# An attention and maxout kernel: columns in token order, and one store per output tile of 128 rows

## The chip, the cores and the metric

The kernel runs on one core of one Trainium2 chip. The metric is the device time of one execution, in microseconds (us). "Before" is the kernel as it stood, "after" the same kernel with the change.

## What is computed

```python
def _attn_ref(q, k, v):                        # q, k, v: 8 x 12 x 448 x 64, float32
    scale = 1.0 / np.sqrt(q.shape[-1])
    scores = scale * np.matmul(q, k.transpose(0, 1, 3, 2))
    m = np.max(scores, axis=-1, keepdims=True)
    e = np.exp(scores - m)
    attn = e / (np.sum(e, axis=-1, keepdims=True) + np.exp(-m) + 1e-09)
    return np.matmul(attn, v).astype(np.float32)

def _moe_ref(x, w1, w2, w3, w_out):            # x: 3584 x 768, all weights 768 x 768
    h = np.maximum(np.maximum(x @ w1, x @ w2), x @ w3)
    return (h @ w_out).astype(np.float32)

# reference: x = the attention's output, one row for each (batch, token), the 12 heads side by side
```

Softmax has one added to its denominator in the unshifted form: e^s / (sum of e^s + 1).

## The kernel before, in words

**Attention.** Eight batches of 448 tokens, each with 12 heads in three groups of four: 24 groups. A group's q, k and v are loaded so that partition p holds the seven tokens 7p to 7p+6 of a head (`rows_of`), and the kernel works through seven "chunks" j, where chunk j holds the tokens 7p+j. So in every tile whose columns are queries, column j*64+p belongs to token 7p+j: the columns are in chunk order. For each group TensorE makes the scores (`visit`, L297), ScalarE the exponentials (L321), VectorE the sums over chunks (`sum_e`, L331), and TensorE the denominators (`den_group`) and the products with v (`num_group`, L345). `norm_group` (L400, VectorE) then multiplies the product, in PSUM, by the reciprocal of the denominator, and writes 448 columns of `xT[b]`, the transposed x of batch b in fp16: twice for each group. The three groups of batch 0 run in two parts of three and four chunks, and `num_part` (L493) writes their x.

**Feed-forward.** `hT`, a tile of fp16 for two batches (896 columns), holds the transposed h. `up_piece` makes 448 columns of it for one block of 128 features and one of the three weights: six matmuls, then an eviction that copies (first weight) or takes the maximum in place (L523, L526). `up_part` does it for batch 0 by parts, two feature blocks at a time (matmuls L537, evictions L546 and L548). `out_piece` makes 128 rows by 384 columns of the output: matmuls of six h blocks (L560 for batch 0, L786 when mixed into the later attention), an eviction that divides by 256 into `o_sb` (L568 or L576), and after the second half `store` (L586). The attention's steps and the pieces are mixed by hand-written lists and by a planner that books costs in steps; TensorE executes its queue strictly in that order.

**The store.** A tile of 128 columns of h holds two runs of 64 columns in chunk order, so `store` issues two transfers of 64 rows, and the rows of each lie seven apart in the output:

```python
for n in range(2):
    b, j = divmod(2 * t + n, NJ)
    rows = out[(b0 + b) * S : (b0 + b + 1) * S].rearrange("(p j) m -> j p m", j=NJ)
    engines[n].dma_start(out=rows[j][:, cols], in_=src[half(n)])
```

**The end.** The last four batches are made in two pairs by a scheme of seven products for eight (`late_pair`; matmuls L1038). `out_unit(m)` gives two output tiles, `o1` (tile m) and `o2` (tile 3+m), in halves of 384 columns. Its `put` evicts a half from PSUM: on ScalarE (L1162), on VectorE with a temporary added (L1168), or, where `late` is set in the last pair, on VectorE without one (L1164). In the last pair many halves are stored as soon as they are evicted; of the two transfers, the first is issued on SyncE and the second on GpSimd or, where `late` is set, on ScalarE. `last_tile` makes tile 6 of a pair with plain matmuls (L1240) and evicts it on VectorE (L1212); in the last pair its second half comes as two quarters, and its second transfers are on ScalarE. The order of all this is one written list that ends with the last pair's unit D[2] and tile e.

SyncE's queue carries, besides the stores, 16 transposing transfers of q and k (L288). GpSimd issues all other loads.

Of the kernel before, what the change touches and what calls it, by code (L numbers as in the profile page):

```python
# [13 lines left out]
ALU = mybir.AluOpType  # L14
ts = bass.ts

MMDT = FP16
LAMBDA = 256.0
# [4 lines left out]
def kernel(  # L23
# [11 lines left out]
    nc = tc.nc  # L35

    B, H, S, D = q.shape
    NTOK, DM = out.shape
    DFF = moe_w1.shape[1]
    KC = 64  # L40
    NJ = S // KC
# [29 lines left out]
    banks = ExitStack()  # L71
# [9 lines left out]
    def single(name, shape=(512,), dtype=FP32):  # L81
        return ps1.tile([128, *shape], dtype, tag="bank1", name=name)
# [21 lines left out]
    def half(n):  # L104
        return slice(n * KC, n * KC + KC)
# [54 lines left out]
    for _ in range(WQ):  # L160
        for r in range(2):
            for c in range(2):
                nc.tensor.matmul(
                    out=warm[r][c * KC : c * KC + KC, 0:WN],
# [25 lines left out]
    state = {}  # L190
# [8 lines left out]
    def book(engine, cost, ready=0.0):  # L199
        given[engine] = max(given[engine], ready, steps[0]) + cost  # L200
        return given[engine] + SEEN
# [135 lines left out]

    xT = {}

    def new_x(b):  # L340
        xT[b] = xt_pool.tile([128, NDC, S], MMDT, tag="xT", name="xT")

# [54 lines left out]
    def norm_group(i, banks, r):  # L397
        book("dve", 2.8)
        b, g = groups[i]
        nc.vector.tensor_tensor(  # L400
            out=xT[b][:, 2 * g + r, :], in0=banks[r][:, 0:S], in1=state[i]["rb"][:, r], op=ALU.mult
        )


# [95 lines left out]
    hT = {}  # L500
# [27 lines left out]
    def up_part(b, fp, i, part, bank=None):  # L528
        if fp == 0 and i == 0 and part == 0:
            hT[b // 2] = ht_pool.tile([128, NFC, 2 * S], MMDT, tag="hT", name="hT")  # L530
        q0, q1 = PARTS[part]
        nq = (q1 - q0) * KC
        dst = hT[b // 2][:, 2 * fp : 2 * fp + 2, q0 * KC : q1 * KC]
        p_i = single("p_i") if bank is None else bank
        for j in range(2):
            for dc in range(NDC):
                nc.tensor.matmul(  # L537
                    out=p_i[:, ts(j, nq)],
                    lhsT=w_sb[i][:, dc, ts(2 * fp + j, 128)],
                    rhs=xT[b][:, dc, q0 * KC : q1 * KC],  # L540
                    start=(dc == 0),
                    stop=(dc == NDC - 1),
                )
        src = p_i[:, 0 : 2 * nq].rearrange("p (j q) -> p j q", j=2)
        if i == 0:
            nc.vector.tensor_copy(out=dst, in_=src)  # L546
        else:
            nc.vector.tensor_tensor(out=dst, in0=dst, in1=src, op=ALU.max)  # L548

    NH = 2  # L550
    NW = DM // NH
    NT = 2 * S // 128
# [26 lines left out]
        if nh == NH - 1:  # L579
            store(2 * bp, t, o_sb, slice(0, DM))  # L580

    def store(b0, t, src, cols, engines=(nc.sync, nc.sync)):
        for n in range(2):
            b, j = divmod(2 * t + n, NJ)
            rows = out[(b0 + b) * S : (b0 + b + 1) * S].rearrange("(p j) m -> j p m", j=NJ)
            engines[n].dma_start(out=rows[j][:, cols], in_=src[half(n)])  # L586

    pieces = []

# [54 lines left out]
    for i, part in ((0, 0), (1, 0), (0, 1), (1, 1), (2, 0), (2, 1)):  # L644
        for fp in range(NFC // 2):
            pieces.append((up_part, (0, fp, i, part), 1.0))
# [96 lines left out]
    late = []  # L743
# [230 lines left out]
    for i in range(MID, NI + 1):  # L974
        for op, j, w in ORDER if i > MID else ORDER[4:]:
# [23 lines left out]
            if op == "N":  # L999
                for_pair()  # L1000
                pair = num_group(i - 1)
                n = turn[0] % 2
                steps[0] += 7
                t = max(steps[0] + 1, state[i - 1]["recip"])
# [6 lines left out]
    while spare:  # L1011
        f, a = spare.pop(0)
# [19 lines left out]
    def part(name, n):  # L1032
        return tail.tile([128, n], FP32, tag=name, name=name, bufs=3 if name == "p7" else 4)

    def product(u, which, lhs, rhs, n, start):
        bank = u[which][:, 0:n]
        for k in range(3):
            nc.tensor.matmul(  # L1038
                out=bank,
                lhsT=lhs(k),  # L1040
                rhs=rhs(k),
                start=start and k == 0,
                stop=k == 2,
                skip_group_check=True,
            )
        return bank

    def bank_of(u, which):
        u[which] = tps[taken[0] % 8].tile([128, 512], FP32, tag="tbank", name="bank_" + which)
        taken[0] += 1  # L1050

    def late_pair(p):

        b0 = 2 * p
        ending = p == B // 2 - 1
# [91 lines left out]
        def out_unit(m):  # L1147
            t = comb[3]
            u = {}
            r0 = slice(m * 128, m * 128 + 128)  # L1150
            r1 = slice(NT3 + m * 128, NT3 + m * 128 + 128)

            def copy(name, bank):
                u[name] = part(name, S)[:, 0:NW]
                nc.scalar.activation(out=u[name], in_=bank, func=AF.Copy, scale=1.0 / LAMBDA)

            def put(o, nh, bank, other=None, late=m == 2 and ending):

                engines = nc.sync, nc.scalar if late else nc.gpsimd
                dst = u[o][:, ts(nh, NW)]  # L1160
                if other is None and not late:
                    nc.scalar.activation(out=dst, in_=bank, func=AF.Copy, scale=1.0 / LAMBDA)  # L1162
                elif other is None:
                    nc.vector.tensor_scalar(  # L1164
                        out=dst, in0=bank, scalar1=1.0 / LAMBDA, scalar2=None, op0=ALU.mult
                    )
                else:
                    nc.vector.scalar_tensor_tensor(  # L1168
                        out=dst, in0=bank, scalar=1.0 / LAMBDA, in1=other, op0=ALU.mult, op1=ALU.add
                    )  # L1170
                t = {"o1": m, "o2": 3 + m}[o]
                if ending and (o == "o1" or m == 0):
                    store(b0, t, dst, ts(nh, NW), engines)
                elif nh == (1 if o == "o1" else 0):
                    store(b0, t, u[o], slice(0, DM), engines if ending else (nc.sync, nc.sync))

            def p1():
                bank_of(u, "a")
                copy("p1", product(u, "a", lambda k: hp[:, k, r0], lambda k: wout_sb[:, k, 0:NW], NW, True))

            def p2():
                bank_of(u, "s")
                u["o1"] = tail.tile([128, DM], FP32, tag="o1", name="o1", bufs=5)
                bank = product(u, "s", lambda k: hp[:, 3 + k, r0], lambda k: wout_sb[:, 3 + k, 0:NW], NW, True)
                put("o1", 0, bank, u["p1"], False)

            def p6():
                copy("u2", product(u, "a", lambda k: sh[1][:, k, r0], lambda k: t[:, 1, k], NW, False))

            def p7():  # L1190
                copy("p7", product(u, "s", lambda k: sh[2][:, k, r0], lambda k: t[:, 2, k], NW, True))

            def p5():
                u["o2"] = tail.tile([128, DM], FP32, tag="o2", name="o2", bufs=3)
                put("o2", 1, product(u, "a", lambda k: sh[0][:, k, r0], lambda k: t[:, 0, k], NW, False), u["p7"])

            def p4():
                put("o2", 0, product(u, "s", lambda k: hp[:, 3 + k, r1], lambda k: t[:, 3, k], NW, False), u["u2"])

            def p3():  # L1200
                bank = product(u, "a", lambda k: sh[3][:, k, r0], lambda k: wout_sb[:, 3 + k, NW:DM], NW, False)
                put("o1", 1, bank, late=ending and m > 0)

            return [p1, p2, p6, p7, p5, p4, p3]

        def last_tile():

            o_last = tail.tile([128, DM], FP32, tag="o_last", name="o_last")

            def columns(c0, c1, cuts, end=None):  # L1210
                def done(bank):
                    nc.vector.tensor_scalar(  # L1212
                        out=o_last[:, c0:c1],
                        in0=bank[:, 0 : c1 - c0],
                        scalar1=1.0 / LAMBDA,
                        scalar2=None,
                        op0=ALU.mult,
                    )
                    if end is not None:
                        store(b0, NT - 1, o_last[:, end], end, (nc.sync, nc.scalar if ending else nc.sync))  # L1220

                return plain(hp, NT - 1, c0, c1, cuts, done)

            return (
                columns(0, NW, (3,), slice(0, NW) if ending else None)
                + columns(NW, NW + NW // 2, ())
                + columns(NW + NW // 2, DM, (), slice(NW if ending else 0, DM))
            )
# [54 lines left out]
    g = last_tile()  # L1283
# [61 lines left out]
```

## Time and profile before

| What | Value |
| --- | --- |
| median of 3 runs | 315.86 us (315.54, 315.86, 320.21) |
| the profiled execution | 315.63 us |
| its span in the profile | 313.9 us |
| TensorE matmuls, busy | 300.7 us (96% of the span) |
| VectorE, busy | 247.7 us (79%) |
| ScalarE, busy | 230.7 us (73%) |
| GpSimd, busy | 83.0 us (26%) |
| bytes moved by transfers | 40.58 MB |
| granted TensorE clock | 0.999 |

The span is the time from the first to the last thing that the profile records; the execution's own time is 1.73 us longer. In the profile's rows PE is TensorE's matmuls, PEld its weight loads, DVE VectorE, ACT ScalarE, POOL GpSimd, and SPq and ACTq the queues of SyncE and ScalarE where they issue transfers. A row of a group names line, engine, operation, what it writes and reads, and the number of instructions, then the total busy time in us and the mean of one in ns, then the idle time before them and what ended it. A row of a wait has the waiter, what it waited for, the total in us, the number of times and the longest. A row of the timeline begins with start and duration in us.

### The profile page before, as it was taken

The numbers are of one execution on the slowest core, as the hardware profiler recorded it, in microseconds if no ns is written. First come the engines' busy times: TensorE is split into PE (matmuls) and PEld (weight loads), VectorE is DVE, ScalarE is ACT, GpSimd is POOL, SyncE is SP. The second block draws the span as 40 slices with busy tenths as digits, with TensorE's granted clock in tenths as the row PEclk, the third lists the DMA queues.
The fourth block names the chain that finished last, engine by engine and source line by source line (L and its number), as shares of the span: only waits on it lengthen the run. The fifth ranks groups of instructions, "written<-read, shape, count | busy, mean of one in ns | idle before, by whom it ended". The sixth has DMA issues, their size and how long they took to land.

```text
span 313.9 us, 11772 instructions
## 1 busy us (share of the span) xinstructions
PE 300.7 (96%) x5132; PEld 213.2 (68%) x5132; DVE 247.7 (79%) x456; ACT 230.7 (73%) x315; POOL 83.0 (26%) x137
## 2 busy tenths in 40 slices
PE   7779999999999999999999999999999999999992
PEld 5557777658999778777666767777765555556551
DVE  3667598999889788888887898877857994989753
ACT  1999859987888988889888899999845457451540
POOL 8644441220434333434332434010000000000220
PEclk9999999999999999999999999999999999999999
DMA  8999999699778999889999999950004000002687
GB/s 152 196 203 205 208 207 203 102 158 176 95 118 138 188 210 143 99 127 180 204 150 145 100 194 217 143 90 2 4 2 102 1 2 0 0 2 70 179 241 215
DMA packets 59348, 40.58 MB, mean 129 GB/s; under 512 B 32256, under 2 KB 56288, under 8 KB 59296
## 3 DMA queue, kind: packets, MB, share of 16 engines
q0 software_dynamic: 25104, 21.80, 47.8%
q1 hardware_dynamic: 33648, 17.21, 26.6%
q8 instruction: 40, 0.66, 0.8%
q10 hardware_dynamic: 544, 0.82, 0.8%
q14 instruction: 12, 0.10, 0.1%
HBM read 42.47 MB, written 11.01 MB: 170 GB/s over the span
## 4 chain that ended last, share of the span: by engine, by line
PE 85%; ACT 6%; DVE 3%; issue 2%; DMA 1%; DVEq 0%; ACTq 0%
PE piece L786 35%; PE bank_a L1038 11%; PE stp L297 9%; PE bank_s L1038 8%; PE av L345 8%; PE p_i L537 4%; ACT eTp L419 3%; PE bank_a L1240 2%; PE piece L537 2%; ACT eT L321 2%; PE den L345 2%; DMA first_k<-in_k_dram 1%; PE piece L560 1%; DVE eS L331 1%; PE num L345 1%
## 5 line engine op out<-in xcount | busy, mean ns | idle before, releaser
L321 ACT ACTIVATE eT<-stp 128x896 f16<-128x896 f32 x147 | 128.9, 920 | 20.5 <-PE stp L297 20.4
L786 PE MATMUL piece<-xT,w 64*64 64x448 f16 x1968 | 120.6, 349 | 0.4 <-DVE xT L400 0.3
L786 PEld LDWEIGHTS <-w 64*64 64x64 f16 x1968 | 76.8, 107 | 18.1 <-issue 1.1
L331 DVE TENSOR_TENSOR eS<-eS,eT 128x896 f16<-128x896 f16 x105 | 64.9, 618 | 3.4 <-ACT eT L321 0.2
L297 PE MATMUL stp<-qkT 64*64 64x448 f16 (+2 forms) x756 | 63.4, 334 | 3.0 <-issue 0.9
L526 DVE TENSOR_TENSOR hT<-hT,piece 128x448 f16<-128x448 f16 x52 | 32.2, 619 | 13.1 <-PE piece L786 8.1
L297 PEld LDWEIGHTS <-qkT 64*64 64x64 f16 x756 | 28.6, 105 | 17.4 <-issue 6.8
L345 PE MATMUL av<-eT,ld_v 64*64 64x448 f16 x588 | 32.2, 349 | 0.0
L400 DVE TENSOR_TENSOR xT<-av,rb 128x448 f16<-128x448 f32 x42 | 24.2, 618 | 8.3 <-PE av L345 6.9
L345 PEld LDWEIGHTS <-ld_v 64*64 64x64 f16 x756 | 26.1, 107 | 6.5 <-issue 0.5
L114 POOL DMA_DIRECT2D ld_v<-in_v_dram x28 | 16.8, 600 | 51.5 <-PE stp L297 31.7
L786 PE MATMUL piece<-w,hT 64*64 64x384 f16 x456 | 29.3, 323 | 0.1
L586 POOL DMA_DIRECT2D out_dram<-o x7 | 3.8, 538 | 93.7 <-DVE o L1168 92.1
L114 POOL DMA_DIRECT2D ld_k<-in_k_dram x26 | 15.4, 596 | 39.1 <-PE stp L297 34.7
L365 ACT ACTIVATE rb<-den 128x896 f32<-128x896 f32 x21 | 19.3, 917 | 8.2 <-PE den L345 8.1
L419 ACT ACTIVATE eTp<-stp 128x768 f16<-128x768 f32 (+3 forms) x24 | 18.1, 821 | 6.0 <-PE stp L297 5.9
L537 PEld LDWEIGHTS <-w 128*128 128x128 f16 x216 | 18.7, 98 | 5.0 <-issue 3.5
L1038 PEld LDWEIGHTS <-comb 128*128 128x128 f16 x132 | 12.9, 98 | 12.2 <-issue 0.4
L786 PEld LDWEIGHTS <-hT 64*64 64x64 f16 x456 | 18.5, 107 | 3.7 <-issue 0.3
L372 ACT ACTIVATE rb<-rb 128x896 f32<-128x896 f32 x21 | 20.0, 952 | 0.2
L537 PE MATMUL p_i<-xT,w 128*128 128x192 f16 (+1 forms) x156 | 16.5, 257 | 0.0
L114 POOL DMA_DIRECT2D ld_q<-in_q_dram x26 | 15.7, 616 | 1.1 <-issue 1.1
(103 smaller groups left out, 404.9 us busy)
## 6 DMA issues: line engine op xcount, KB each, us to landing
out_dram<-o_sb SPq DMA_DIRECT2D x28, 192.0 KB, 4.6
ld_v<-in_v_dram POOLq DMA_DIRECT2D x28, 112.0 KB, 4.1
ld_k<-in_k_dram POOLq DMA_DIRECT2D x26, 112.0 KB, 3.0
ld_q<-in_q_dram POOLq DMA_DIRECT2D x26, 112.0 KB, 4.0
out_dram<-o SPq DMA_DIRECT2D x14, 192.0 KB, 3.1
ld_q<-in_q_dram POOLq DMA_DIRECT2D x11, 224.0 KB, 9.2
ld_k<-in_k_dram POOLq DMA_DIRECT2D x10, 224.0 KB, 9.3
ld_v<-in_v_dram POOLq DMA_DIRECT2D x10, 224.0 KB, 8.5
```

The source lines that it names most:

```text
L114: return eng.dma_start(out=dst[half(hp)].rearrange("p s j d -> p s (j d)"), in_=rows_of(name, i)[half(hp)])
L297: mm = nc.tensor.matmul(out=out[half(c), r], lhsT=qkT[half(r), 0, j, h], rhs=qkT[half(r), 1, q0:q1, h], start=True, stop=True,)
L321: nc.scalar.activation(out=st["eT"][:, j], in_=stp[:, :, 0:S], func=AF.Exp, scale=scale, bias=-math.log(EDIV))
L331: nc.vector.tensor_tensor(out=st["eS"], in0=st["eT"][:, 0] if j == 1 else st["eS"], in1=st["eT"][:, j], op=ALU.add,)
L345: nc.tensor.matmul(out=outs[r][half(c)], lhsT=weights(r, c), rhs=moving(r, c), start=start, stop=stop,)
L372: nc.scalar.activation(out=st["rb"], in_=st["rb"], func=AF.Exp, bias=math.log(LAMBDA), scale=-1.0)
L400: nc.vector.tensor_tensor(out=xT[b][:, 2 * g + r, :], in0=banks[r][:, 0:S], in1=state[i]["rb"][:, r], op=ALU.mult)
L419: nc.scalar.activation(out=eT[:, j0 : j0 + n].rearrange("p j r q -> p r j q"), in_=stp[:, :, 0 : n * nq].rearrange("p r (j q) -> p r j q", ...
L526: nc.vector.tensor_tensor(out=dst, in0=dst, in1=p_i[:, 0:S], op=ALU.max)
L537: nc.tensor.matmul(out=p_i[:, ts(j, nq)], lhsT=w_sb[i][:, dc, ts(2 * fp + j, 128)], rhs=xT[b][:, dc, q0 * KC : q1 * KC], start=(dc == 0), ...
L786: nc.tensor.matmul(out=p["bank"][half(c), 0:w], lhsT=lhs(k, r, c), rhs=rhs(k, r), start=(r == p["first"] and k == 0), stop=(r != p["first" ...
L1038: nc.tensor.matmul(out=bank, lhsT=lhs(k), rhs=rhs(k), start=start and k == 0, stop=k == 2, skip_group_check=True,)
```

## The change

- `norm_group` writes the columns of x in the order of the tokens: column q*7+j in place of j*64+q. The values and the operation stay; the write becomes seven runs of 64 elements, each with a step of seven elements.
- `num_part` still writes batch 0's x in chunk order; `up_part` turns the order when it evicts h, for `hT[0]`.
- Everything behind (sums of x and h, matmuls, evictions of the output) keeps its instructions, on columns that are now in token order.
- `store` issues one transfer of 128 rows, which lie one behind the other in the output, on SyncE.
- In the last pair, `put` evicts every half without a temporary on ScalarE, where two were on VectorE. Tile 5 (the `o2` of m = 2) is stored in two halves, not whole. GpSimd stores nothing any more, and ScalarE issues one store: the second half of tile 2.

```diff
--- before.py
+++ after.py
@@ -337,6 +337,11 @@
 
     xT = {}
 
+
+
+    def by_chunk(t):
+        return t.rearrange("p (q j) -> p j q", j=NJ)
+
     def new_x(b):
         xT[b] = xt_pool.tile([128, NDC, S], MMDT, tag="xT", name="xT")
 
@@ -398,7 +403,10 @@
         book("dve", 2.8)
         b, g = groups[i]
         nc.vector.tensor_tensor(
-            out=xT[b][:, 2 * g + r, :], in0=banks[r][:, 0:S], in1=state[i]["rb"][:, r], op=ALU.mult
+            out=by_chunk(xT[b][:, 2 * g + r]),
+            in0=banks[r][:, 0:S].rearrange("p (j q) -> p j q", j=NJ),
+            in1=state[i]["rb"][:, r].rearrange("p (j q) -> p j q", j=NJ),
+            op=ALU.mult,
         )
 
 
@@ -530,7 +538,7 @@
             hT[b // 2] = ht_pool.tile([128, NFC, 2 * S], MMDT, tag="hT", name="hT")
         q0, q1 = PARTS[part]
         nq = (q1 - q0) * KC
-        dst = hT[b // 2][:, 2 * fp : 2 * fp + 2, q0 * KC : q1 * KC]
+        dst = hT[0][:, 2 * fp : 2 * fp + 2, 0:S].rearrange("p f (q j) -> p f j q", j=NJ)[:, :, q0:q1]
         p_i = single("p_i") if bank is None else bank
         for j in range(2):
             for dc in range(NDC):
@@ -541,7 +549,7 @@
                     start=(dc == 0),
                     stop=(dc == NDC - 1),
                 )
-        src = p_i[:, 0 : 2 * nq].rearrange("p (j q) -> p j q", j=2)
+        src = p_i[:, 0 : 2 * nq].rearrange("p (f j q) -> p f j q", f=2, q=KC)
         if i == 0:
             nc.vector.tensor_copy(out=dst, in_=src)
         else:
@@ -579,11 +587,8 @@
         if nh == NH - 1:
             store(2 * bp, t, o_sb, slice(0, DM))
 
-    def store(b0, t, src, cols, engines=(nc.sync, nc.sync)):
-        for n in range(2):
-            b, j = divmod(2 * t + n, NJ)
-            rows = out[(b0 + b) * S : (b0 + b + 1) * S].rearrange("(p j) m -> j p m", j=NJ)
-            engines[n].dma_start(out=rows[j][:, cols], in_=src[half(n)])
+    def store(b0, t, src, cols, engine=nc.sync):
+        engine.dma_start(out=out[b0 * S + t * 128 :][0:128, cols], in_=src)
 
     pieces = []
 
@@ -1154,25 +1159,19 @@
                 u[name] = part(name, S)[:, 0:NW]
                 nc.scalar.activation(out=u[name], in_=bank, func=AF.Copy, scale=1.0 / LAMBDA)
 
-            def put(o, nh, bank, other=None, late=m == 2 and ending):
-
-                engines = nc.sync, nc.scalar if late else nc.gpsimd
+            def put(o, nh, bank, other=None):
                 dst = u[o][:, ts(nh, NW)]
-                if other is None and not late:
+                if other is None:
                     nc.scalar.activation(out=dst, in_=bank, func=AF.Copy, scale=1.0 / LAMBDA)
-                elif other is None:
-                    nc.vector.tensor_scalar(
-                        out=dst, in0=bank, scalar1=1.0 / LAMBDA, scalar2=None, op0=ALU.mult
-                    )
                 else:
                     nc.vector.scalar_tensor_tensor(
                         out=dst, in0=bank, scalar=1.0 / LAMBDA, in1=other, op0=ALU.mult, op1=ALU.add
                     )
                 t = {"o1": m, "o2": 3 + m}[o]
-                if ending and (o == "o1" or m == 0):
-                    store(b0, t, dst, ts(nh, NW), engines)
+                if ending and (o == "o1" or m != 1):
+                    store(b0, t, dst, ts(nh, NW), nc.scalar if t == 2 and nh == 1 else nc.sync)
                 elif nh == (1 if o == "o1" else 0):
-                    store(b0, t, u[o], slice(0, DM), engines if ending else (nc.sync, nc.sync))
+                    store(b0, t, u[o], slice(0, DM))
 
             def p1():
                 bank_of(u, "a")
@@ -1182,7 +1181,7 @@
                 bank_of(u, "s")
                 u["o1"] = tail.tile([128, DM], FP32, tag="o1", name="o1", bufs=5)
                 bank = product(u, "s", lambda k: hp[:, 3 + k, r0], lambda k: wout_sb[:, 3 + k, 0:NW], NW, True)
-                put("o1", 0, bank, u["p1"], False)
+                put("o1", 0, bank, u["p1"])
 
             def p6():
                 copy("u2", product(u, "a", lambda k: sh[1][:, k, r0], lambda k: t[:, 1, k], NW, False))
@@ -1199,7 +1198,7 @@
 
             def p3():
                 bank = product(u, "a", lambda k: sh[3][:, k, r0], lambda k: wout_sb[:, 3 + k, NW:DM], NW, False)
-                put("o1", 1, bank, late=ending and m > 0)
+                put("o1", 1, bank)
 
             return [p1, p2, p6, p7, p5, p4, p3]
 
@@ -1217,7 +1216,7 @@
                         op0=ALU.mult,
                     )
                     if end is not None:
-                        store(b0, NT - 1, o_last[:, end], end, (nc.sync, nc.scalar if ending else nc.sync))
+                        store(b0, NT - 1, o_last[:, end], end)
 
                 return plain(hp, NT - 1, c0, c1, cuts, done)
```

## The prediction

> **What bounds the kernel now.** I read the page first: busy shares, then the chain that ended last.
>
> ```profile
> span 313.9 us, 11772 instructions
> PE 300.7 (96%) x5132; PEld 213.2 (68%) x5132; DVE 247.7 (79%) x456; ACT 230.7 (73%) x315; POOL 83.0 (26%) x137
> ...
> PE 85%; ACT 6%; DVE 3%; issue 2%; DMA 1%; DVEq 0%; ACTq 0%
> ```
>
> TensorE is the bound: 96% busy, 85% of the chain. Transfers are 1% of it, although their engines are busy for most of the span. A change pays only if TensorE gets shorter, waits less, or the work after its last matmul ends sooner. Next, the busy time of each engine over the steady stretch and over the last eight microseconds:
>
> ```profile
> core 0: us, PE busy (x) PEld busy (x) DVE busy (x) ACT busy (x) POOL busy (x), PEclk, DMA share, GB/s
> 75.00:225.00 150.00, 149.89 (x3182) 116.83 (x3176) 126.81 (x237) 130.49 (x165) 47.65 (x80) 1.00 0.88 136
> ...
> 306.00:310.00 4.00, 2.15 (x20) 1.51 (x17) 2.43 (x6) 0.00 (x0) 0.00 (x0) 1.00 0.96 267
> 310.00:314.00 4.00, 0.00 (x0) 0.00 (x0) 0.00 (x0) 0.00 (x0) 0.00 (x0) 0.91 0.46 155
> ```
>
> From 75 to 225 us TensorE loses 0.1 us in 150, and VectorE is idle for 23. From 306 on the transfer engines are 96% busy. Third, the waits of TensorE's weight loads, and the group of the instruction that the change alters most:
>
> ```profile
> PEld L297 <- DVE xT L400: 3.0, 11, 0.4
> ```
>
> ```profile
> L400 DVE TENSOR_TENSOR xT<-av,rb 128x448 f16<-128x448 f32 x42 | 24.2, 618 | 8.3 <-PE av L345 6.9 <-ACT eT L321 1.0
> ...
> L493 DVE TENSOR_TENSOR xT<-num,rb 128x256 f16<-128x256 f32 x6 | 2.3, 417 | 1.2 <-ACT rb L466 1.2
> ...
> L493 DVE TENSOR_TENSOR xT<-num,rb 128x192 f16<-128x192 f32 x6 | 1.9, 352 | 2.3 <-ACT rb L466 2.3
> ```
>
> The normalisation comes in pairs (21 of them). In 11 pairs its end is what the next score matmuls wait for (0.27 us each), since it frees their bank: a longer L400 reaches TensorE at once. Last, the end in order of time:
>
> ```profile
> 306.39 0.56 DVE L1168 SCALAR_TENSOR_TENSOR o<-bank_a,p 128x384 f32<-128x384 f32 x1
> 306.87 0.55 DVE L1168 SCALAR_TENSOR_TENSOR o<-bank_s,u 128x384 f32<-128x384 f32 x1
> ...
> 306.98 0.84 SPq L586 DMA_DIRECT2D out_dram<-o_last  x1
> ...
> 307.49 0.66 PE L1240 MATMUL bank_a<-w,hT 128*128 128x192 f16 x6
> 307.69 0.56 DVE L1164 TENSOR_SCALAR o<-bank_a 128x384 f32<-128x384 f32 x1
> 307.91 1.58 SPq L586 DMA_DIRECT2D out_dram<-o  x2
> 308.19 0.36 DVE L1212 TENSOR_SCALAR o_last<-bank_a 128x192 f32<-128x192 f32 x1
> 308.85 1.11 ACTq L586 DMA_DIRECT2D out_dram<-o_last  x1
> 309.68 0.80 SPq L586 DMA_DIRECT2D out_dram<-o_last  x1
> ```
>
> TensorE ends at 308.15, the last eviction at 308.55, but SyncE, still busy with earlier stores, begins the last store at 309.68: 1.13 us late. That store lands 3.4 us after its issue begins, at 313.1; 0.8 us later the span ends.
>
> **The change part by part.** (1) The 42 normalisations (L400) write the same 448 values with a step of 7 fp16 elements, 14 bytes. Reads, count and order stay. The three widths above fit a line: (618-352)/(448-192) = 1.04 ns an element plus 152 ns. So the operation already moves one element per 1.04 ns, and a write of one element at a time may cost the same wherever it lands. No row of this trace writes single elements apart; the bounds are 618 ns and one doubled element time, 618+466 = 1084 ns. I take 618: the row is the same operation at its slow pace, with nothing packed that a step could undo. Upper end: rival D. A gain is excluded, as no work is removed.
>
> [...]
>
> (2) The 18 evictions of batch 0's h (L546, L548) write with the same step, and 12 read it back too. Same bounds: 555 or 680 ns as now, up to 0.4 or 0.53 us more each. I take 0, for the same reason.
>
> (3) One wait is added. Batch 0's first output tile now needs columns from every part of h, so its fifth weight load (line 560) waits for the last maximum:
>
> ```profile
> 59.28 1.14 PE L560 MATMUL piece<-w,hT 128*128 128x384 f16 x6
> ...
> 59.50 0.68 DVE L548 TENSOR_TENSOR hT<-hT,piece 128x512 f16<-128x512 f16 x1
> ```
>
> The six matmuls take 0.19 us each, so the fifth starts at 60.04; the maximum ends at 60.18. TensorE waits 0.15 us, about 0.2 with the signal. Behind it stand the next scores, at 60.35 and for them ScalarE. Bounds 0 (0.3 us of unexplained idle stands before those scores) and 0.7 (the whole operation in front). I take +0.2. The other matmuls keep their order and waits.
>
> (4) Stores. Outside the end, 28 transfers of 64 rows become 14 of 128 on SyncE. The transposes behind them start earlier, but nothing waits for those: no row of TensorE's waits names them. 0. In the end, 26 issues on SyncE, 7 on GpSimd and 5 on ScalarE become 19 on SyncE and 1 on ScalarE. A 64-row issue takes 466 ns at least, 584 median, up to 853. No 128-row store is in the trace; the nearest is one load of the start, 64 rows with two runs each:
>
> ```profile
> L114 SPq DMA_DIRECT2D first_k<-in_k_dram x1: 771/771/771, 0.7 to 0.7; - x1
> ```
>
> I take 0.77 us, bounds 0.47 (cost by instruction) and 1.17 (two median short issues). SyncE's last four stores are ready at 306.29, 306.95, 307.42 and 308.55. At 0.77 they begin at 306.3, 307.1, 307.8 and 308.6: the last is not late, 1.1 us gained. At 1.0 it begins at 309.3, 0.4 gained; at 1.17, at 309.8, 0.1 lost. (The 16 stores from 292.3 on make a second limit, 292.3 plus 15 issues: 303.9 at 0.77, 309.9 at 1.17.) But transfers are nearly saturated there, and the last one carries 192 KB in place of 96. Six halves of 197 KB become ready after 306.2: 1.18 MB at some 300 GB/s are 3.9 us. With about 1 us from ready to moving, bytes flow until some 311.2, against 312.1 now. I take half of the 1.1 us: -0.5, bounds -1.1 and +0.2.
>
> (5) The second halves of the last pair's tiles 1 and 2 (L1164, two) go from VectorE to ScalarE: 0.49 for 0.55 us. ScalarE is idle from 300.86 to 303.05 and after 305.8, which hides both; without that cover they would delay a temporary by 0.5 us. VectorE's last eviction starts at 308.19 as TensorE lets it. 0. The evictions' waits for a free buffer drop one of two transfers; none cost time. 0.
>
> **Sum.** +0.2 - 0.5 = -0.3 us on the profiled execution, 315.63 (span 313.9 and 1.73 around it): 315.3. The median of the runs is 315.86, 0.2 above; the three runs lie 315.54 to 320.21. I give 315.3.
>
> **Rivals.** B, *the saturated end*: store bandwidth and not the late issue sets the end, -0.5 becomes 0, and the wait of (3) stays: 315.8. For it: 96% from 306 to 310. Against: 1.1 us in which a finished tile had not been asked for.
>
> C, *long issues*: a 128-row issue costs more than two short ones, say 1.3 us under load, and SyncE falls behind from 292.3 on: the last store begins at 292.3 + 15 x 1.3 = 311.8, +2.1 for -0.5: 317.9. It decides from 1.16 us. For it: 1109 ns on ScalarE while SyncE issued too. Against: 96 and 192 KB stores both reach 466.
>
> D, *the step halves the element rate*, the other side. Place: L400. Price: 2 x 0.466 = 0.93 us a pair. TensorE waits already in 11 pairs, so at least 10.2; at most 21 x 0.93 = 19.6. (2) adds 18 x 0.45 = 8 us of VectorE, mostly beside idle time. I take 13: 328. It passes 2% (6.3 us) from 0.3 us a pair if all count, 0.57 if 11 do: L400 at 770 to 900 ns. For it: no row shows such a write. Against: the slow pace of the row.
>
> E, *whole tiles drain faster*: the last bytes at the 356 GB/s of the best slices, 1.18 MB in 3.3 us, so 0.6 more: 314.7. For it: the digits of the last slices vary between 169 and 384 GB/s. Against: halves overlap, and 300 GB/s is already reached.
>
> [...]
>
> That the change does less than it says is B.
>
> **How the numbers follow.** Forecast 0.47, B 0.20, C 0.08, E 0.09, D 0.16. Range 313.8 to 318.5: below, the forecast with (4) at its full gain and E, 314.1, and a little; above, C with 0.7 in place of 0.2 for (3), 318.4, which also holds a small cost of the step, up to 0.15 us a pair. It leaves out D, 0.16. Two per cent, 6.3 us, is about what a measurement of this kernel can tell from no change. Only D goes beyond, nearly always: slower 0.15, same 0.83, and 0.02 for a gain over 2%, which no case here gives.
>
> **What would show it.** Right: L400 at 618 ns within 10, its wait row still near 3 us, the last store on SyncE beginning before 309.3, its issue under 1 us, span 313 to 314. Wrong: L400 over 770 and its wait row over 10 us (D); issues of 1.3 us (C); the last store prompt but landing at 313 (B).

## The result, and the profile after

The change made the kernel 28% slower. Medians here and below are of all runs; ratios and their intervals count only the runs in the faster of two states that the executions show.

| | before | after |
| --- | --- | --- |
| median of 6 runs each | 316.66 us | 405.85 us (401.08 to 406.98) |
| ratio, 95% interval | | 1.2785 [1.2704, 1.2865] |
| span of the profiled execution | 313.9 us | 404.0 us |
| granted TensorE clock | 0.999 | 0.916 |

Below are the head of the page of after, its clock digits and the first line of its chain. The lines of the code have moved: L400 is L405, L493 is L501, L537 is L545, L546 and L548 are L554 and L556, L560 is L568, L586 is L591, L786 is L791.

```profile
span 404.0 us, 11725 instructions
PE 335.5 (83%) x5132; PEld 215.4 (53%) x5132; DVE 319.1 (79%) x454; ACT 235.2 (58%) x317; POOL 79.0 (20%) x130
...
PEclk9999968888989888989899889898898899999999
...
PE 60%; DVE 22%; issue 9%; ACT 5%; DMA 2%; POOL 1%; DVEq 0%; POOLq 0%; ACTq 0%
```

VectorE was 3% of the chain and is 22%. TensorE runs the same 5132 matmuls and is busy for 34.8 us longer: the digits of its clock fall to 6 in the sixth slice and are 8 or 9 from there to the end of the attention. The groups whose write the change turned, and one that it left alone (L501), with the mean of one in ns after the comma:

```profile
L405 DVE TENSOR_TENSOR xT<-av,rb 128x448 f16<-128x448 f32 x42 | 76.6, 1988 | 9.4 <-PE av L350 7.8 <-ACT eT L321 1.5
...
L556 DVE TENSOR_TENSOR hT<-hT,piece 128x512 f16<-128x512 f16 x4 | 8.7, 2180 | 1.8 <-PE piece L545 1.8
L556 DVE TENSOR_TENSOR hT<-hT,p_i 128x384 f16<-128x384 f16 x5 | 8.3, 1661 | 0.7 <-PE p_i L545 0.7
...
L501 DVE TENSOR_TENSOR xT<-num,rb 128x256 f16<-128x256 f32 x6 | 2.2, 416 | 0.1
```

Every turned write takes some three times as long: 1988 ns for 618, 1661 for 553, 2180 for 682. The waits of TensorE and of its weight loads (total, times, longest):

```profile
PE stp L297 <- DVE xT L405: 38.0, 17, 2.5
...
PEld L297 <- DVE xT L405: 35.5, 13, 2.9
...
PEld L568 <- DVE hT L556: 4.4, 1, 4.4
```

The score matmuls wait for a bank, 17 times, 2.2 us a time; before, 11 weight loads waited 0.27 us each. Where the 90 us lie is seen in the windows. Each kernel's span is cut at the start of the first normalisation and at the end of the last; the first stretch is the feed-forward of batch 0 between the attention's first groups. Before, then after:

```profile
20.00:58.40 38.40, 37.18 (x710) 28.45 (x705) 29.62 (x54) 32.19 (x41) 14.29 (x21) 1.00 1.17 194
58.40:233.40 175.00, 174.46 (x3630) 133.11 (x3629) 149.37 (x279) 150.36 (x188) 51.46 (x86) 1.00 0.85 132
233.40:313.90 80.50, 74.41 (x449) 41.13 (x443) 58.93 (x103) 34.94 (x67) 3.76 (x7) 1.00 0.28 79
```

```profile
20.00:75.30 55.30, 43.34 (x711) 31.14 (x706) 49.56 (x56) 32.90 (x41) 14.14 (x21) 0.88 0.81 135
75.30:326.90 251.60, 204.82 (x3655) 133.48 (x3653) 202.12 (x279) 153.39 (x188) 51.19 (x86) 0.89 0.59 92
326.90:404.00 77.10, 72.61 (x417) 40.35 (x417) 57.82 (x101) 36.01 (x69) 0.00 (x0) 1.00 0.22 83
```

The three stretches differ by +16.9, +76.6 and -3.4 us, 90.1 in all. In the middle one TensorE's idle time goes from 0.5 to 46.8 us, and its matmuls are busy for 204.8 us in place of 174.5, at a mean clock of 0.89. So there are two losses: 46 us of waiting and 30 us of a slower clock. The first stretch has both too: 10.7 us more idle time and 6.2 us more busy time, at 0.88.

The mean hides how the clock falls. One of the 17 waits, and the clock (the third number from the end) in the two stretches behind it:

```profile
301.86 0.38 PE L297 MATMUL stp<-qkT 64*64 64x448 f16 x4 [2.31 <-DVE xT L405]
```

```profile
302.90:306.10 3.20, 3.20 (x40) 1.74 (x36) 2.49 (x5) 2.04 (x3) 0.00 (x0) 0.50 0.00 0
306.30:316.30 10.00, 7.69 (x168) 4.68 (x163) 7.67 (x10) 5.79 (x7) 0.00 (x0) 1.00 0.01 2
```

From 302.8 to 306.2 us, 3.4 us, the granted clock is half, and then whole again until the next pair. The middle of the span has 16 such stretches. At half speed each loses 1.7 us, by this estimate 27 us of the 30.

The last stretch got shorter. Half of its 3.4 us lies ahead of the last matmul, where fewer matmuls are left (417 records for 449); the other half is the end. In order of time:

```profile
399.29 0.66 PE L1239 MATMUL bank_a<-w,hT 128*128 128x192 f16 x6
...
399.98 0.36 DVE L1211 TENSOR_SCALAR o_last<-bank_a 128x192 f32<-128x192 f32 x1 [0.62 <-PE bank_a L1239]
...
400.37 0.33 SPq L591 DMA_DIRECT2D out_dram<-o_last  x1
```

The last matmul ends at 399.95, the eviction at 400.34, and the last store begins 0.03 us later, where it began 1.13 us late before. From the last matmul to the end of the span are 4.05 us; before they were 5.75.

### The profile page after: what moved, and what is told of

The parts are those of the page before. It is cut to its first block, busy times and chain, and to the rows that moved or that the text cites. A ratio compares the mean times of both kernels' runs of the same rounds, so it can differ in the third digit from the quotient of the medians.

```text
span 404.0 us, 11725 instructions
## 1 busy us (share of the span) xinstructions
PE 335.5 (83%) x5132; PEld 215.4 (53%) x5132; DVE 319.1 (79%) x454; ACT 235.2 (58%) x317; POOL 79.0 (20%) x130
## 3 DMA queue, kind: packets, MB, share of 16 engines
q1 hardware_dynamic: 34080, 18.39, 19.6%
## 4 chain that ended last, share of the span: by engine, by line
PE 60%; DVE 22%; issue 9%; ACT 5%; DMA 2%; POOL 1%; DVEq 0%; POOLq 0%; ACTq 0%
PE piece L791 25%; DVE xT L405 13%; PE bank_a L1043 9%; PE stp L297 8%; PE bank_s L1043 6%; PE av L350 5%; DVE eS L331 3%; DVE hT L556 2%; PE bank_a L1239 2%; DMA ld_q<-in_q_dram 2%; PE p_i L545 2%; PE piece L545 1%; ACT eTp L427 1%; ACT eT L321 1%; PE den L350 1%
## 5 line engine op out<-in xcount | busy, mean ns | idle before, releaser
L321 ACT ACTIVATE eT<-stp 128x896 f16<-128x896 f32 x147 | 131.3, 916 | 103.8 <-PE stp L297 100.9
L791 PE MATMUL piece<-xT,w 64*64 64x448 f16 x1968 | 138.2, 391 | 2.5 <-DVE xT L405 2.4
L297 PE MATMUL stp<-qkT 64*64 64x448 f16 (+2 forms) x756 | 68.7, 371 | 44.5 <-DVE xT L405 38.0
L791 PEld LDWEIGHTS <-w 64*64 64x64 f16 x1968 | 73.8, 119 | 39.0 <-issue 13.5
L405 DVE TENSOR_TENSOR xT<-av,rb 128x448 f16<-128x448 f32 x42 | 76.6, 1988 | 9.4 <-PE av L350 7.8
L331 DVE TENSOR_TENSOR eS<-eS,eT 128x896 f16<-128x896 f16 x105 | 69.2, 659 | 3.6 <-ACT eT L321 0.4
L297 PEld LDWEIGHTS <-qkT 64*64 64x64 f16 x756 | 27.2, 115 | 65.6 <-DVE xT L405 35.5
L791 PE MATMUL piece<-w,hT 64*64 64x384 f16 x456 | 33.3, 360 | 0.0
L545 PEld LDWEIGHTS <-w 128*128 128x128 f16 x216 | 20.8, 106 | 8.4 <-issue 5.8
L791 PEld LDWEIGHTS <-hT 64*64 64x64 f16 x456 | 20.5, 120 | 5.2 <-issue 0.7
L545 PE MATMUL p_i<-xT,w 128*128 128x192 f16 (+1 forms) x156 | 17.4, 264 | 2.6 <-DVE hT L554 2.4
L331 DVE TENSOR_TENSOR eS<-eT 128x896 f16<-128x896 f16 x21 | 13.5, 642 | 2.8 <-ACT eT L321 2.8
```

The source lines that it names most:

```text
L297: mm = nc.tensor.matmul(out=out[half(c), r], lhsT=qkT[half(r), 0, j, h], rhs=qkT[half(r), 1, q0:q1, h], start=True, stop=True,)
L321: nc.scalar.activation(out=st["eT"][:, j], in_=stp[:, :, 0:S], func=AF.Exp, scale=scale, bias=-math.log(EDIV))
L331: nc.vector.tensor_tensor(out=st["eS"], in0=st["eT"][:, 0] if j == 1 else st["eS"], in1=st["eT"][:, j], op=ALU.add,)
L405: nc.vector.tensor_tensor(out=by_chunk(xT[b][:, 2 * g + r]), in0=banks[r][:, 0:S].rearrange("p (j q) -> p j q", j=NJ), in1=state[i]["rb"][ ...
L545: nc.tensor.matmul(out=p_i[:, ts(j, nq)], lhsT=w_sb[i][:, dc, ts(2 * fp + j, 128)], rhs=xT[b][:, dc, q0 * KC : q1 * KC], start=(dc == 0), ...
L791: nc.tensor.matmul(out=p["bank"][half(c), 0:w], lhsT=lhs(k, r, c), rhs=rhs(k, r), start=(r == p["first"] and k == 0), stop=(r != p["first" ...
```

## The experiments

Each expectation names its theories itself. Unless an interval is given, a time is that of one run, the profiled one.

### The operations alone: m1_steps

This kernel holds only the disputed instructions, six of each: 448 columns out of PSUM, multiplied by a tile in SBUF, written with a growing step. ScalarE's copies and 64 matmuls with each kind of operand follow. The lines are shortened.

```diff
+ tt(out=h_seven[:, 0 : N * 7 : 7], in0=ps[:, 0:N], in1=rb, op=mul)   # and steps 1 to 32
+ tt(out=h_runs.rearrange("p (q j) -> p j q", j=7), in0=ps..., in1=rb..., op=mul)   # as the change writes
+ tt(out=h_psread..., in0=ps[:, 0:N].rearrange("p (j q) -> p q j", j=7), in1=rb..., op=mul)
```

> Each operation by itself, six times in a row, nothing beside it; the attention and the feed-forward are left out. Contiguous multiply of 448 columns from PSUM into fp16: 618 ns as in the kernel before. Theory A (each element that VectorE writes apart from its neighbour costs a turn of its own, some 4 ns): the seven runs with a step of 7 take 1900 to 2000 ns here too, and so do single runs with any fp16 step from 2 or 3 up; the reads may be strided at 618. Theory B (the distance in bytes sets the price): the time grows with the step up to 8 or so and fp32 reaches the same price at half the step. Theory C (in the kernel the strided writes collide with other engines' accesses): 618 here at every step. If the seven runs and not the step were the cost, the single run with step 7 would be 618. On ScalarE contiguous 545; strided write near 545 if the cost belongs to VectorE, over 1500 if it belongs to the memory. TensorE with the 64x448 moving operand read in steps of 256 bytes: 0.19 us a matmul in sequence if the read is free, 0.4 or more if it is not.

The groups: fp16 writes with steps of 1, 2, 3, 4, 7 and 8 elements; the change's own seven runs; a contiguous write with both reads turned, and with only the read of PSUM turned; an fp32 write with a step of 4; an fp16 read with a step of 7; and ScalarE's contiguous and turned write.

```profile
L48 DVE TENSOR_TENSOR h_one<-ps,rb 128x448 f16<-128x448 f32 x6 | 3.7, 613 | 0.2
L52 DVE TENSOR_TENSOR h_two<-ps,rb 128x448 f16<-128x448 f32 x6 | 3.9, 655 | 0.2
L56 DVE TENSOR_TENSOR h_three<-ps,rb 128x448 f16<-128x448 f32 x6 | 5.4, 902 | 0.2
L60 DVE TENSOR_TENSOR h_four<-ps,rb 128x448 f16<-128x448 f32 x6 | 6.9, 1152 | 0.2
L72 DVE TENSOR_TENSOR h_seven<-ps,rb 128x448 f16<-128x448 f32 x6 | 11.5, 1921 | 0.2
L76 DVE TENSOR_TENSOR h_eight<-ps,rb 128x448 f16<-128x448 f32 x6 | 13.0, 2166 | 0.2
L95 DVE TENSOR_TENSOR h_runs<-ps,rb 128x448 f16<-128x448 f32 x6 | 11.5, 1922 | 0.2
L98 DVE TENSOR_TENSOR h_reads<-ps,rb 128x448 f16<-128x448 f32 x6 | 5.5, 912 | 0.2
L101 DVE TENSOR_TENSOR h_psread<-ps,rb 128x448 f16<-128x448 f32 x6 | 3.7, 623 | 0.2
L117 DVE TENSOR_TENSOR f_four<-ps,rb 128x448 f32<-128x448 f32 x6 | 5.7, 943 | 0.2
L131 DVE TENSOR_TENSOR s_seven<-ps,h_seven 128x448 f16<-128x448 f32 x6 | 5.0, 835 | 0.2
L137 ACT ACTIVATE a_cont<-ps 128x448 f16<-128x448 f32 x6 | 3.3, 543 | 178.6 <-DVE s_eight L134 178.5
L140 ACT ACTIVATE a_runs<-ps 128x448 f16<-128x448 f32 x6 | 11.7, 1957 | 0.2
```

The time grows with the step up to 8 elements, 16 bytes, and then stops: steps of 9 to 32 take 2060 to 2150 ns. Counted in lines of 16 bytes, the distance at which the growth ends, steps 3, 4, 7 and 8 touch 168, 224, 392 and 448 different ones, and 152 ns + 4.5 ns a line, an estimate fitted to these rows, gives 908, 1160, 1916 and 2168, each within 8 ns of its row. Step 2 enters 112 lines, 656 by this fit for 655; contiguous columns enter 56, and there the pace of one element per 1.04 ns is the longer of the two (618 for 613). The evictions of batch 0 in after fit too: 384 values, 336 lines, 1664 ns for 1661; 512 values, 448 lines, 2168 for 2180. So counting the lines entered fits the rows, counting the elements does not, and a constant price for a separated element is refuted by the growth from 902 to 2166. (A price by the distance between two elements, capped at 16 bytes, gives the same numbers; no run parts the two, and none shows what a line is.) The split into seven runs costs nothing (1922 for 1921). ScalarE pays the same (1957 for 543), so the price is not VectorE's alone. Reading fp16 or writing fp32 in steps costs by the same count some 1.75 ns a line (835 and 943), reading PSUM in steps nearly nothing (623 for 613).

### The stores alone: e1_store_only

x and h stay in chunk order, the rest of the change is kept; the rows of each batch come out in chunk order. Of the edit, the normalisation; h is as under e2.

```diff
-            out=by_chunk(xT[b][:, 2 * g + r]),
...
+            out=xT[b][:, 2 * g + r, :], in0=banks[r][:, 0:S], in1=state[i]["rb"][:, r], op=ALU.mult
```

> The changed kernel with contiguous writes of x and h, so that columns stay in chunk order; the stores, the evictions and the queues at the end are those of the change (the turn to token order is left out, so the output's rows within a batch stand in another order). Theory A (all of the loss comes from the strided writes, and the end gains what the changed kernel's own end shows: 4.05 us from the last matmul to the end of the span, before 5.75): span 312.2 and time 314.0 to 314.6, ratio 0.995. Rival (the saturated end takes the gain back, as the prediction's case B): 315.6, ratio 1.000. Rival (whole stores cost something elsewhere): over 318.

The ratio is 0.9984 [0.9949, 1.0018] over 12 runs against 17 of before (317.08 and 316.50 us): no difference; the 0.995 of theory A lies at the interval's edge. The whole loss is thus in the order of the columns. In the profile the end is 4.1 us long, as in after; the gain of 1.7 us against before's profile is not visible in the times.

### The two halves of the loss: e2_norm_only and e3_part_only

The first turns only the 42 normalisations, the second only batch 0's 18 evictions; both keep the stores, and some rows come out in another order.

```diff
# e2: batch 0's evictions as before
-        dst = hT[0][:, 2 * fp : 2 * fp + 2, 0:S].rearrange("p f (q j) -> p f j q", j=NJ)[:, :, q0:q1]
+        dst = hT[b // 2][:, 2 * fp : 2 * fp + 2, q0 * KC : q1 * KC]
...
# e3: the normalisations as before
-            out=by_chunk(xT[b][:, 2 * g + r]),
...
+            out=xT[b][:, 2 * g + r, :], in0=banks[r][:, 0:S], in1=state[i]["rb"][:, r], op=ALU.mult
```

> As the kernel with the stores only, but the 42 normalisations write with the step of 7 elements; batch 0's evictions of h stay contiguous. Theory A (additive, by VectorE's time): 42 x 1.37 us = 57.5 us of the 88.4 lost, and a little for the granted clock: 372 to 382 us, clock about 0.93. Rival (most of the loss is batch 0's evictions and what they delay): under 345. Rival (the lower clock is the cause, not the stall): the clock stays 0.91 and the time near 400.

> As the kernel with the stores only, but batch 0's 18 evictions of h write with the step of 7 elements; the normalisations are contiguous. VectorE works 21.4 us longer before 80 us. Theory A (additive): 405.9 - 387.1 = 18.8 us more than the stores only, 334 to 337. Rival (hidden beside ScalarE's and the loads' work of the start): under 325.

e2 took 387.14 us (clock 0.929), above the 372 to 382 expected; e3 took 334.91 (clock 0.98), as expected. Against before's medians beside them, 316.5 and 316.6, they lose 70.6 and 18.3 us, 88.9 together; the change loses 89.2. So about 71 us come from the normalisations and 18 from batch 0's evictions. In before one pair of normalisations keeps its banks for 1.15 us, in e2 for 3.65 (less than two means, since the records of two instructions in a row overlap):

```profile
58.43 1.15 DVE L400 TENSOR_TENSOR xT<-av,rb 128x448 f16<-128x448 f32 x2
```

```profile
60.13 3.65 DVE L405 TENSOR_TENSOR xT<-av,rb 128x448 f16<-128x448 f32 x2
```

Its window from the first normalisation to the last shows TensorE idle for 44.8 us and busy for 29 us more than before:

```profile
60.10:308.30 248.20, 203.45 (x3656) 131.87 (x3653) 201.11 (x279) 154.37 (x188) 51.25 (x86) 0.90 0.58 93
```

### Time without the step: e4_delay and e5_twice

If only VectorE's time matters, contiguous writes that are merely repeated must cost the same. e4 does each normalisation three times over, e5 twice, both in chunk order.

```diff
+        for _ in range(3):        # e5: range(2)
+            nc.vector.tensor_tensor(
+                out=xT[b][:, 2 * g + r, :], in0=banks[r][:, 0:S], in1=state[i]["rb"][:, r], op=ALU.mult
+            )
```

> As the kernel with the stores only, contiguous writes, but each normalisation is made three times over (1854 ns in place of 618; the strided one took 1988). Theory A (only VectorE's time counts, wherever it goes): 1.24 / 1.37 = 0.9 of the loss of the kernel with strided normalisations alone, so 365 to 376 us, and the granted clock falls as much, to some 0.93, with no strided write in it. Rival (the strided write also slows the other engines' accesses to the same memory, as the 659 ns of the sums in place of 618 may say): well under 0.9 of the loss, say 345 to 355, and the clock near 0.97.

> As the kernel with the stores only, but each normalisation is made twice over, contiguous: a pair 1.24 us longer, where three times over made it 2.47 us longer and cost 75 us (3.6 us a pair). Theory A (waits of TensorE cost themselves, and past some length the granted clock falls for a while and costs more): 21 x 1.24 = 26 us and a clock of 0.98 or more: 338 to 345. Rival (the cost is proportional, the clock falls with every wait): half of 75, 353, clock 0.96.

e4 took 391.75 us at a clock of 0.926, above the 365 to 376 expected. The expectation compared the means, 1.24 us added to an operation in e4 and 1.37 in e2; but by the pairs e4 adds 2.63 us and e2 2.50, so e4 loses more, 75.3 us for 70.6. Its pair and its wait:

```profile
205.26 3.78 DVE L406 TENSOR_TENSOR xT<-av,rb 128x448 f16<-128x448 f32 x6
```

```profile
PE stp L297 <- DVE xT L406: 40.4, 17, 2.6
```

No write of e4 has a step, and its 3.78 us a pair cost as much for each added microsecond as the 3.65 of e2, and the clock as well. So the step costs the kernel nothing here beyond VectorE's time, and a lasting effect of the stepped layout on what reads x, a third possibility, is not needed. The rise of the sums (L331) from 618 to 659 ns, which the expectation took as a possible sign of colliding accesses, is of the sums right behind a stepped write: their records begin before that write ends (in after one at 105.78, while the pair ends at 106.11). In after the 29 sums behind one take 773 to 791 ns, the other 97 at most 627. e5 took 340.38 us at 0.995, as expected, its longest wait 1.7 us: 23.9 us lost for 21 x 1.31 = 27.5 us of added VectorE time.

```profile
59.31 2.46 DVE L406 TENSOR_TENSOR xT<-av,rb 128x448 f16<-128x448 f32 x4
```

### The clock: e6_filled

As e2, but 18 matmuls of 64 columns, whose result nobody reads, are queued ahead of the waiting scores in 17 of the groups. They lie in the wait, and shorten TensorE's pauses: 0.70 us for the 18.

```diff
+                for _ in range(18):
+                    nc.tensor.matmul(
+                        out=p["bank"][:, S:512], lhsT=ident16, rhs=warm16[:, 0 : 512 - S], ...
```

> The kernel with strided normalisations alone (387.1 us), with 18 idle matmuls of 64 columns in the queue ahead of the scores that wait for the normalised bank, in 17 of the 21 groups; they write columns that nobody reads. They lie inside TensorE's wait of some 2.5 us, so by themselves they cost nothing. Theory A (the granted clock falls because TensorE stands idle for over 2 us at a time; from the first to the last normalisation that made its busy time 203 us in place of 174): the clock rises to 0.97 or more, and most of those 29 us come back: 360 to 368 us. Rival (the clock falls for another reason, or the busy time is a mere reading of late matmuls): 385 to 390, clock 0.93. Rival (the idle matmuls displace work): over 392.

367.12 us, within the 360 to 368 expected and 20.0 less than e2, with some 12 us of work more. Its clock digits, the groups of the feed-forward's matmuls in after and in this kernel, its longest wait row, and one pause, which in e2 lasts 2.48 us at the same place:

```profile
PEclk9999999899999999998999999999999999999999
```

```profile
L791 PE MATMUL piece<-xT,w 64*64 64x448 f16 x1968 | 138.2, 391 | 2.5 <-DVE xT L405 2.4
```

```profile
L791 PE MATMUL piece<-xT,w 64*64 64x448 f16 x1968 | 119.8, 349 | 2.5 <-DVE xT L405 2.4
```

```profile
PE stp L297 <- DVE xT L405: 28.4, 17, 1.9
```

```profile
123.69 0.38 PE L297 MATMUL stp<-qkT 64*64 64x448 f16 x4 [1.86 <-DVE xT L405]
```

The clock is back at 0.991, and the matmul at 349 ns, its time before. From the first normalisation to the last e2's trace has 15 stretches of half clock, this one two. So the lower clock followed from TensorE's pauses, not from the layout of x, which is the same in e2. The loss that is left, 50.6 us against 316.5, is 0.96 of the 52.5 us by which VectorE's 21 pairs grew.

### Token order without the stepped write: v2_both_reads and v3_psum_reads

The write is contiguous and the read of PSUM does the turning. In v2 the reciprocal in SBUF is read in steps as well; in v3 it is already in token order, since ScalarE's operation that makes it reads PSUM in steps too. The edits are shortened. Batch 0 stays in chunk order with stores of 64 rows, for its parts would need stepped writes. v3's output is in the order of the tokens throughout, as the change's is.

```diff
-            out=by_chunk(xT[b][:, 2 * g + r]),
-            in0=banks[r][:, 0:S].rearrange("p (j q) -> p j q", j=NJ),
+            out=xT[b][:, 2 * g + r, :].rearrange("p (q j) -> p q j", j=NJ),
+            in0=banks[r][:, 0:S].rearrange("p (j q) -> p q j", j=NJ),
# v2
+            in1=state[i]["rb"][:, r].rearrange("p (j q) -> p q j", j=NJ),
# v3, and the operation that makes rb
+            in1=state[i]["rb"][:, r].rearrange("p (q j) -> p q j", j=NJ),
+            out=st["rb"].rearrange("p r (q j) -> p r q j", j=NJ),
+            in_=dps[:, :, 0:S].rearrange("p r (j q) -> p r q j", j=NJ),
```

> As the kernel with reads of PSUM in token order, but rb stays in chunk order and the normalisation reads it with a step of 256 bytes from SBUF: 912 ns by itself, +0.59 us for a pair. Theory A (TensorE waits one for one for the end of the pair, in all 21): 315 + 21 x 0.59 = 327, with the granted clock still 0.99 or more since each wait is short. Rival (slack hides it where TensorE did not wait before, in 10 of 21): 322. Rival (any added wait costs more than itself through the clock): over 332.

> Token order without a strided write. The logarithm of the denominator (ScalarE) reads its bank in PSUM in token order and writes rb contiguously; the normalisation reads the product in PSUM in token order, rb and x are contiguous. Batch 0 stays in chunk order as before, and its four tiles are stored in halves of 64 rows; the rest is the change. From the operations by themselves: a strided read of PSUM by VectorE costs 623 for 613 ns, by ScalarE 592 for 543 for 448 columns, so 21 x 0.1 = 2 us of ScalarE, which is 73% busy. Theory A (only the strided write to SBUF costs): L400's successor stays at 620 to 630 ns, the time is that of the kernel with the stores only, ratio 0.994 to 1.002, and after TensorE's last matmul 4.1 us remain, before 5.75. Rival (in the full kernel, with TensorE writing PSUM beside it, the strided read slows too): the normalisation above 800 ns and the time above 325.

v2: the operation takes 924 ns, and the kernel 326.3 us at a full clock, as expected. v3: 316.52 us over 12 runs, ratio 0.9997 [0.9964, 1.003]. Its normalisation, and the operation on ScalarE, which takes 917 ns as before:

```profile
L370 ACT ACTIVATE rb<-den 128x896 f32<-128x896 f32 x21 | 19.3, 917 | 8.2 <-PE den L350 8.1
...
L408 DVE TENSOR_TENSOR xT<-av,rb 128x448 f16<-128x448 f32 x42 | 24.2, 618 | 8.3 <-PE av L350 6.9 <-ACT eT L321 1.0
```

So the order of the columns of batches 1 to 7 can be had for nothing, and it gives back all that the change lost; it does not beat the kernel before by an amount that was measured.

### Where the end's gain goes: b2_before and b3_before

e1 and v3 have a shorter end, but not a shorter time. Two more profiles of the kernel before, without an edit, ask whether its start is earlier than theirs.

> The kernel before, profiled again. In its first profile the first matmul of h began at 20.1 us, in the six changed kernels at 20.6 to 21.7. Theory A (the start varies by itself and hides the end's gain of 1.65 us): between 20.5 and 22 here, and 5.7 to 5.8 us from the last matmul to the end of the span again. Rival (the change makes the start later): 20.1 again, within 0.2.

> The kernel before once more, as b2: Theory A 20.5 to 22 us; rival 20.1 within 0.2; the end 5.7 to 5.8 us after the last matmul in both.

They took 316.23 and 317.2 us; their ends are 5.8 and 5.9 us long, against 3.6 to 4.1 with the new stores. The first matmul of h starts at 20.6 and 20.5 us (20.1 in the first profile of before), in after at 20.3, in e1 at 21.1 and in v3 at 21.7. From there to the last matmul v3 takes 288.0 us, the three profiles of before 288.1, 288.1 and 289.1, so nothing between the start and the end takes v3's gain back. The first normalisation starts at 58.4, 59.0 and 59.8 us in the three profiles of before, and between 58.8 and 60.1 in the seven with the change's stores and batch 0 as before. That scatter is nearly as large as the gain of 1.7 to 2.1 us. Whether the new stores really start the work later stays open.

## Why the prediction was wrong

**Step (1) failed, and (2) with it.** It sized the 14-byte step at 0, with 1084 ns as the upper end; the operation takes 1988, and the wait row of the weight loads behind it went from 3.0 to 35.5 us: the sign that the prediction had named for D. The reasoning was that an operation at one element per 1.04 ns has "nothing packed that a step could undo". The rows of m1_steps show that there is something to undo: the same 448 values take 613 ns side by side, 902 with a step of 3 and 1921 with a step of 7. The straight line through 352, 417 and 618 ns was measured on contiguous writes alone and could not show this. My upper bound, one doubled element time, came from no row that had a step, and so was no bound.

The type counts as well as the distance: 8 bytes apart, the 448 values are written in 623 ns for 622 as fp32, and in 1152 for 613 as fp16.

**Rival D had the place, and a third of the price.** The scores do wait for the bank that L405 frees. It counted 0.93 us a pair where 2.5 were added, and it had no clock. The runs that change only the normalisations make a series (losses against 316.5 us; one run each):

| run | one pair, us (before 1.15) | added in 21 pairs | lost | lost / added | clock |
| --- | --- | --- | --- | --- | --- |
| v2 | 1.77 | 13.0 | 9.8 | 0.75 | 1.000 |
| e5 | 2.46 | 27.5 | 23.9 | 0.87 | 0.995 |
| e6 | 3.65 | 52.5 | 50.6 | 0.96 | 0.991 |
| e2 | 3.65 | 52.5 | 70.6 | 1.34 | 0.929 |
| e4 | 3.78 | 55.2 | 75.3 | 1.36 | 0.926 |

While the clock holds, 0.75 to 0.96 of VectorE's added time is lost; where it falls, more than all of it. D's span of 10.2 to 19.6 us for 0.93 a pair agrees with that series; its threshold of 770 to 900 ns also does, as v2 at 924 ns lost 3%.

**(2)** was taken as 0 beside idle time: the 18 evictions grew by 1.1 to 1.5 us each, 23 us by the rows of e3, and e3 lost 18.3 us. Not all of that is waiting: in the first stretch of after 10.7 us are TensorE's idle time and 6.2 the slower clock.

**(3)** was right in place and wrong in size: 4.4 us for 0.2. The maximum in front takes 2.32 us by itself and begins only at 78.56 us, when the first pair of normalisations, begun at 75.26, is nearly done.

**(4)** had the right mechanism. The last store is not late, and the end is 1.7 us shorter, beyond the upper bound of 1.1. The mis-sized term is the issue: 0.33 us for 128 rows in a plain block of the output (332 ns at the median, 425 at most among the stores of the end), where 0.77 was taken and 0.47 was the lower bound. Of the 1.7 us, 1.1 is the store that is no longer late and 0.5 its shorter issue (0.33 for 0.80 us); only 0.1 is left for the faster drain of rival E. C is thereby wrong for this kernel, and so is the mechanism of B; but B's figure, no gain in the time, is what e1 and v3 measured. What of the gain reaches the time, e1 puts between -1.6 and +0.6 us (0.9949 and 1.0018 of 316.5), so the forecast gain of 0.3 us could not have been told from none. **(5)** cost nothing that a profile shows; v3, which has it, has the time of before.

## What to carry to other kernels

Time an fp16 write to SBUF with the step that it will have, not by a fit to contiguous writes: here the reordering made the operation 3.2 times as long (1988 ns for 618; 3.5 times with a step of 8 in m1_steps, 2166 for 613), and it cost nothing where it was put into the read of PSUM instead (618 ns in v3). An instruction that frees a bank on which TensorE waits cost this kernel most of its added time (0.75 to 0.96 of it), and more than all of it (1.34) where TensorE's pauses grew from at most 1.9 us (e6) to 2.1 to 2.5 in most groups (e2), since then the clock went too (0.929 for 0.991). A bound from rows that lack the feature in dispute is no bound; give the rival that says so a wide price.

## What the runs showed of the hardware

- In m1_steps VectorE's fp16 writes with steps of 3 and 7 took 902 and 1921 ns for 613, by an estimate 4.5 ns for each 16 bytes entered; its fp32 write with a step of 4 took 943 and its fp16 read with a step of 7 835, some 1.75 ns by the same estimate. The two prices were not expected to differ, and no run tells why.
- VectorE and ScalarE read PSUM in steps of 256 bytes in little more time than side by side (623 for 613 ns, 592 for 543, in m1_steps).
- In m1_steps the same 64 matmuls ran with a contiguous moving operand and with one in steps of 256 bytes, in 3.19 and 12.28 us. The clock was whole for the first and 0.86 in the mean for the second, which by an estimate accounts for 1.7 us of the 12.28:

```profile
186.76 3.19 PE L156 MATMUL p_cont<-mv,wt 64*64 64x448 f16 x64
189.79 12.28 PE L154 MATMUL p_str<-mv,wt 64*64 64x448 f16 x64
```

```profile
186.80:189.70 2.90, 2.90 (x68) 1.76 (x64) 0.00 (x0) 2.84 (x3) 0.00 (x0) 1.00 0.02 6
190.00:201.80 11.80, 11.80 (x64) 2.47 (x60) 0.00 (x0) 8.71 (x9) 0.00 (x0) 0.86 0.00 0
```

- From 11 us to the last matmul the traces of this kernel grant a clock of 1.0 or of 0.5, the latter for 3.4 or 6.8 us at a time (in after 16 times 3.4 and twice 6.8). From the first normalisation to the last e2 has 17 pauses of 1.9 to 2.5 us between its matmuls and 15 stretches at 0.5, 0.90 in the mean; e6, with pauses of at most 1.9 us, has two; e5, with at most 1.3 us, has one. So in e2 it fell with pauses of at most 2.5 us, though not after every one; in after too the pauses of 2.3 us from 183.0 and of 2.4 from 261.4 have no stretch at 0.5 right behind them.
- SyncE issued a transfer of 128 rows that lie one behind the other in 0.33 us at the median (after), one of 64 rows that lie seven apart in 0.47 us at least and 0.59 at the median (before). In v3 the last of the eight 64-row stores of batch 0's tiles has its rows one behind the other and took 0.59 us as well, so their place alone does not make the difference.
